# Late slots of three blocks and of one and a half in turn, and the low half of a weight split written one split later

## The chip, the cores and the metric

The kernel runs on one core of one Trainium2 chip. The metric is the device time of one execution in microseconds (us): 579.85 us is the median of three runs before the change (578.74 to 580.92). One further execution was recorded by the hardware profiler. It took 577.57 us, of which 575.6 us lie between the first and the last instruction; this is the span in which all positions below are given, counted from its start.

## The reference

Two stages follow each other. The first is an attention with memory: per batch and head, `phi` is softened over 32 memory columns, `k` and `v` are summed into 32 memory rows with these weights, and the 576 queries attend to the 32 rows. Its output is rearranged to 4608 tokens of 512 numbers. The second is a mixture of 8 experts: each token goes to the one expert with the highest gate value.

```python
e_idx = np.argmax(logits, axis=1)
...
for e in range(E):
    mask = e_idx == e
    h = np.maximum(x[mask] @ w1[e], 0.0)
    ye = h @ w2[e]
    out[mask] = gate_w[mask, None] * eom[mask, e, None] * ye
```

Here `x` is 4608 x 512, `w1[e]` 512 x 1024 and `w2[e]` 1024 x 512, all float32.

## The kernel before

**Slots.** Tokens are sorted by expert into blocks of 128, and blocks of one expert are put together in slots. A slot is a unit of work with one expert's weights. Five early slots (positions 0 to 4) hold three blocks each, from tokens whose attention is finished while attention still runs. The late slots are made when all tokens are routed: five of three blocks (positions 5 to 9), then four "of one and a half" (positions 10 to 13: one block of 128 tokens and a half of 64). Slots of one block exist in the program behind a condition on how many are in use; in the profiled execution none of them runs. Below, a slot of three blocks is called a *triple* and a slot of one and a half a *pair*, as the code's `nb == 3` and `nb == 2`.

**A slot on TensorE.** `several` does one slot. Its first layer runs over four weight tiles `u` = 0 to 3 (each 128 x 1024) and two halves `j`, its second layer over `u` = 4 to 7 and the blocks. Every float32 operand is split in two float32r parts, high and low: `xh` and `xl` for the tokens, `whl[:, 0]` and `whl[:, 1]` for the weights, `hh` and `hl` for the hidden values. A product is then the sum of three matmuls (high by high, low by high, high by low). A pair lays the 192 high and 192 low token columns side by side in one tile, so its first layer needs two matmuls, of 384 columns (line 1212) and of 256 columns (line 1213). After each `u` the sums are evacuated: for a triple by `hh` on ScalarE (line 1221) and `hl` on VectorE (line 1222); for a pair by a longer relay, two copies on ScalarE (1224), two additions on VectorE (1225), the relu on ScalarE (1229) and two subtractions on VectorE (1231).

**Weights.** `Stream` brings them: `fetch` starts the loads of 512 KB tiles on SyncE's queue (line 563) into `raw` buffers, `split` makes the high part by a cast on ScalarE (line 574) and the low part by a subtraction on VectorE (line 575) that needs the cast. The split tiles live in a ring, of ten buffers once attention is over (`settle` adds the last six). `done`, called once for each weight tile that has been used, issues up to two further splits (`PUMP[0]` is 2), so that splits run ahead of their use.

**Tokens.** `gathers` issues the gathering transfers on GpSimd for up to three slots ahead, twelve for a triple and six for a pair, each of a quarter of a row. `turn_x` prepares the tokens of the next slot during the second layer of the present one: four transposes on VectorE (line 1051), four casts to the high part on ScalarE (1058 for a pair, 1069 for a triple) and four subtractions on VectorE (1059 and 1070). The high part `xh` has one buffer, so its first write waits until the present slot's first layer is through.

**Order.** Each engine runs its instructions in the order in which the Python code emits them; nothing is rearranged later. The order of slots is the list `order`, and the place of every split, cast and subtraction in the queues of ScalarE and VectorE follows from where `done`, `nxt` and `hook` are called in `several`.

Of the kernel before, what the change touches and what calls it, by code (L numbers as in the profile page):

```python
# [7 lines left out]
F32 = mybir.dt.float32  # L8
# [4 lines left out]
ALU = mybir.AluOpType  # L13
# [15 lines left out]
NPT, NPP, NSS = 5, 4, 22  # L29
NPE = sum(NPS)  # L30
# [24 lines left out]
PUMP = (2, 1)  # L55
# [11 lines left out]
def attention_moe(tc, phiT, kv, qT, wgo, wall, out):  # L67
    nc = tc.nc
    V, A, G, T = nc.vector, nc.scalar, nc.gpsimd, nc.tensor

    with contextlib.ExitStack() as ctx:
# [385 lines left out]
        env = {}  # L457
# [18 lines left out]
        def force():  # L476
            clock[0] += 1
            (rou if rou.gens else late if late.gens else att).step()

        class Ring:  # L480


            def __init__(self, shape, dt, name):
                self.shape, self.dt, self.name = shape, dt, name
                self.pools, self.turn, self.size = [], [], 0
# [11 lines left out]
        raw = Ring([P, 1024], F32, "w")  # L497
# [5 lines left out]
        slots = []  # L503
        for s in range(NSLOT):
            nb = 3 if s < NPE + NPT else 2 if s < NPE + NPT + NPP else 1
# [3 lines left out]
            else:  # L509
                j = s - NPE  # L510
# [2 lines left out]
            slots.append({"s": s, "nb": nb, "q0": q0, "idx": idx[nm], "rows": rows,  # L513
                          "nm": nm, "quart": s not in WHOLE,
                          "known": False, "listed": False})
        order = slots

        def quarters(z, k):

# [24 lines left out]
        class Stream:  # L544
# [4 lines left out]
            def __init__(self, lo, hi):  # L549
                self.lo = lo  # L550
                self.fetched = self.parted = self.used = 8 * lo
                self.hi, self.w, self.hl = 8 * hi, {}, {}

            def fetch(self):
                while self.fetched < min(self.hi, self.parted + raw.size):
                    z = order[self.fetched // 8]
                    if not z["known"]:
                        return
                    if "e" not in z:
                        z["e"] = nc.sync.value_load(slot[0:1, z["s"]:z["s"] + 1], min_val=0, max_val=E - 1)  # L560
                    w = raw.tile()
                    u = self.fetched % 8
                    nc.sync.dma_start(w[:], wall[bass.ds(z["e"], 1), :, u + 8 * (z["quart"] and u < 4)])
                    self.w[self.fetched] = w
                    self.fetched += 1

            def split(self, ahead):

                self.fetch()
                m = self.parted  # L570
                if m == self.fetched or m >= self.used + ahead:
                    return False
                w, hl = self.w.pop(m), ring.tile()
                A.copy(hl[:, 0], w[:])  # L574
                V.tensor_tensor(hl[:, 1], w[:], hl[:, 0].bitcast(F32), ALU.subtract)  # L575
                self.hl[m] = hl
                self.parted += 1
                self.fetch()
                return True

            def take(self, i, u):
                m = 8 * i + u
                while m not in self.hl:
                    while not order[i]["known"]:
                        force()
                    assert self.split(ring.size)
                return self.hl[m]

            def done(self, n):
# [30 lines left out]
        def bank(shape, key="pa"):  # L620
            t = env[key].tile([P, 512], F32, name="b" + key)
            n = 1
            for x in shape:
                n *= x
            if len(shape) == 1:
                return t[:, 0:n]
            return t[:, 0:n].rearrange("p (a b) -> p a b", a=shape[0])
# [551 lines left out]
        def finish_y(z, k, py):  # L1179
            y = mo.tile([P, DM], F32, name="y", bufs=2)  # L1180
            n = P
            if (z["nb"], k) == (2, 1):

                n = 64
                ya = env["xt"].tile([64, DM], F32, name="ya", bufs=1)
                A.copy(ya[:], py[64:128])
                V.tensor_tensor(ya[:], py[0:64], ya[:], ALU.add)
                py = ya[:]
            A.activation(y[0:n], py[0:n], AF.Copy, scale=z["g"][0:n, k:k + 1] if z["quart"] else z["xg"][:, k, P:P + 1])  # L1189
            G.indirect_dma_start(  # L1190
                out=out, out_offset=bass.IndirectOffsetOnAxis(ap=z["idx"][1][0:n, z["q0"] + k:z["q0"] + k + 1], axis=0),
                in_=y[0:n], in_offset=None, bounds_check=NTOK - 1, oob_is_err=False)

        def several(i, st, nxt, hook):


            z = order[i]
            nb, x, h = z["nb"], z["x"], []
            n_ = nb * P
            for u in range(4):  # L1200
                w = st.take(i, u)
                h_ = mo.tile([P, 2, 3 * P], F32R, name="hh", bufs=4)
                l_ = mo.tile([P, 2, 3 * P], F32R, name="hl", bufs=4) if nb == 3 else None
                sh = mo.tile([P, 2, 192], F32, name="hl", bufs=4) if nb == 2 else None
                for j in range(2):
                    pb = bank([512], "ps")[:, 0:3 * P]
                    n = 0
                    for cc in range(4):
                        o = cc * 256 + j * P
                        if nb == 2:  # L1210

                            T.matmul(pb, w[:, 0, o:o + P], x[0][:, cc], start=(cc == 0), stop=False)  # L1212
                            T.matmul(pb[:, 0:256], w[:, 1, o:o + P], x[0][:, cc, 0:256],  # L1213
                                     start=False, stop=(cc == 3))
                            continue
                        for a, b in PASS:
                            T.matmul(pb, w[:, b, o:o + P], x[a][:, cc, 0:n_],  # L1217
                                     start=(n == 0), stop=(n == 11))
                            n += 1
                    if nb == 3:  # L1220
                        A.activation(h_[:, j], pb, AF.Relu)  # L1221
                        V.scalar_tensor_tensor(l_[:, j], pb, 0.0, h_[:, j].bitcast(F32), ALU.max, ALU.subtract)  # L1222
                    else:
                        A.copy(sh[:, j], pb[:, 192:384])
                        V.tensor_tensor(sh[:, j], pb[:, 0:192], sh[:, j], ALU.add)
                    if j == 0:
                        hook()
                if nb == 2:
                    A.activation(h_[:, :, 0:192], sh[:], AF.Relu)
                    for o, c, m in ((192, P, 64), (256, 0, P)):  # L1230
                        V.scalar_tensor_tensor(h_[:, :, o:o + m], sh[:, :, c:c + m], 0.0,
                                               h_[:, :, c:c + m].bitcast(F32), ALU.max, ALU.subtract)
                h.append((h_, l_))
                st.done(PUMP[0])
                hook()
            py = [bank([DM], "ps") for _ in range(nb)]

            turns = [(u, k) for u in range(4, 8) for k in range(nb)]
            if 8 * i + 8 == st.hi:
                turns.sort(key=lambda t: t[1], reverse=nb == 2)  # L1240
            for step, (u, k) in enumerate(turns):
                w = st.take(i, u)
                for f in range(2):
                    h_, l_ = h[u - 4]
                    if nb == 3:
                        ps = [((h_, l_)[a][:, f, k * P:(k + 1) * P], b) for a, b in PASS]
                    elif k == 0:
                        ps = [(h_[:, f, 256 * a:256 * a + P], b) for a, b in PASS]
                    else:
                        ps = [(h_[:, f, P:256], b) for b in range(2)]  # L1250
                    for n, (a, b) in enumerate(ps):
                        T.matmul(py[k], a, w[:, b, DM * f:DM * f + DM],  # L1252
                                 start=(u == 4 and f == 0 and n == 0),
                                 stop=(u == 7 and f == 1 and n == len(ps) - 1))
                if u == 7:
                    finish_y(z, k, py[k])
                hook()
                if step in TURN[nb]:
                    nxt(TURN[nb].index(step))
                if (step + 1) % nb == 0:  # L1260
                    st.done(PUMP[0])
# [159 lines left out]
```

## Time and profile before

| what | us |
|---|---|
| median of three runs | 579.85 |
| the profiled execution | 577.57 |
| its span | 575.6 |
| TensorE matmul busy in the span | 521.2 |
| VectorE busy | 363.1 |
| ScalarE busy | 288.6 |
| GpSimd busy | 225.6 |

"Busy" sums the time in which at least one instruction of an engine is under way. TensorE's matmuls overlap each other in its pipeline, so a matmul that is listed with 390 ns may follow the one before after 230 ns. The granted clock (PEclk) is 1.00 when TensorE runs at full speed. In the tables by stretches, each row gives the stretch, its length, and for each engine the busy time and the number of instructions; then the granted clock, the share of the DMA engines and GB/s. In rows by time the number in brackets is how long the engine sat idle before, and what released it.

### The profile page before, as it was taken

The page shows a single profiled execution, that of the slowest core. Times are in us where ns is not written, and L with a number is a line of the kernel's source. Part 1 is how long each engine was busy: PE and PEld are TensorE (multiplying, and loading weights), DVE is VectorE, ACT ScalarE, POOL GpSimd, SP SyncE. Part 2 cuts the span into 40 slices and gives each one's busy share as a digit, 9 for nine tenths or more (in the row PEclk, how much of TensorE's full clock was granted, in tenths as well). Part 3 has the DMA queues.
Part 4 walks back from the last instruction along what each step waited for, and adds up shares of the span by engine and source line. Part 5 has one row for each costly group of instructions (what it writes and reads, how often), then busy time and mean ns, then how long its engine had stood idle before and what let it go on. Part 6 is the DMA issues. An engine that isn't in the chain of part 4 may idle for free. (4 is left out here: it accounts for less than half of the span.)

```text
span 575.6 us, 10623 instructions
## 1 busy us (share of the span) xinstructions
PE 521.2 (91%) x3871; PEld 446.5 (78%) x3871; DVE 363.1 (63%) x791; ACT 288.6 (50%) x532; POOL 225.6 (39%) x245
## 2 busy tenths in 40 slices
PE   3788777789899999999999999999999999797894
PEld 2455555469689899898998989899898989696783
DVE  4485989767866559996353555647354545777750
ACT  3476664355345456543434545455453545666651
POOL 2242575740165034402471745547140505352011
PEclk9977989869999999999999999999999999898988
DMA  8999998985457759755564655646465564777101
GB/s 304 414 383 398 408 389 312 317 311 168 116 179 237 234 174 299 259 151 155 184 202 139 206 179 182 193 158 191 138 187 165 177 182 141 202 222 221 49 27 33
DMA packets 41853, 123.53 MB, mean 215 GB/s; under 512 B 10112, under 2 KB 10176, under 8 KB 41408
## 3 DMA queue, kind: packets, MB, share of 16 engines
q1 hardware_dynamic: 35136, 102.71, 55.1%
q0 software_dynamic: 6656, 20.06, 10.0%
q8 instruction: 32, 0.52, 0.4%
q14 instruction: 29, 0.24, 0.1%
HBM read 102.40 MB, written 20.35 MB: 213 GB/s over the span
## 5 line engine op out<-in xcount | busy, mean ns | idle before, releaser
L1252 PE MATMUL bps<-whl,hh 128*128 128x512 f32 x640 | 194.3, 394 | 0.0
L575 DVE TENSOR_TENSOR whl<-w,whl 128x1024 fp32r<-128x1024 f32 x112 | 136.9, 1228 | 66.1 <-ACT whl L574 65.7
L1217 PE MATMUL bps<-xh,whl 128*128 128x384 f32 x640 | 167.1, 338 | 0.0
L1252 PEld LDWEIGHTS bps<-whl,hh 128*128 128x128 f32 x640 | 119.9, 188 | 26.9 <-issue 2.5
L574 ACT CAST whl<-w 128x1024 fp32r<-128x1024 f32 x112 | 116.1, 1044 | 15.5 <-PE bps L1252 15.4
L1217 PEld LDWEIGHTS bps<-xh,whl 128*128 128x128 f32 x640 | 116.8, 189 | 1.2 <-issue 0.6
L1217 PE MATMUL bps<-xl,whl 128*128 128x384 f32 x320 | 107.6, 336 | 0.0
L1252 PE MATMUL bps<-whl,hl 128*128 128x512 f32 x240 | 93.7, 390 | 0.0
L529 POOL DMA_INDIRECT xg<-xs,idx_ql x72 | 84.3, 1171 | 21.9 <-issue 21.3
L1190 POOL DMA_INDIRECT out<-y,idx_ol x23 | 26.0, 1129 | 134.4 <-ACT y L1189 92.8
L1221 ACT ACTIVATE hh<-bps 128x384 fp32r<-128x384 f32 x80 | 39.3, 492 | 76.4 <-PE bps L1217 76.3
L1222 DVE SCALAR_TENSOR_TENSOR hl<-bps,hh 128x384 fp32r<-128x384 f32 x80 | 44.1, 554 | 38.4 <-ACT hh L1221 38.2
L1217 PEld LDWEIGHTS bps<-xl,whl 128*128 128x128 f32 x320 | 60.6, 189 | 0.4
L1212 PE MATMUL bps<-xh,whl 128*128 128x384 f32 x128 | 43.2, 372 | 9.6 <-DVE xh L1059 9.3
L1252 PEld LDWEIGHTS bps<-whl,hl 128*128 128x128 f32 x240 | 45.2, 188 | 8.4
L848 POOL TENSOR_TENSOR ea<-ea,mx 128x512 f32<-128x512 f32 (+1 forms) x20 | 19.2, 961 | 47.7 <-DVE mx L846 43.4
L1213 PE MATMUL bps<-xh,whl 128*128 128x256 f32 x128 | 37.8, 295 | 0.0
L1212 PEld LDWEIGHTS bps<-xh,whl 128*128 128x128 f32 x128 | 26.5, 207 | 12.6 <-DVE xh L1059 12.0
L883 ACT COPY xo<-bpd 128x576 f32<-128x576 f32 x36 | 22.6, 639 | 19.9 <-PE bpd L881 11.6
L966 POOL TENSOR_SCALAR Aw<-iota_row,row 128x128 bf16<-128x128 bf16 x36 | 26.9, 763 | 12.7 <-DVE row L956 12.7
L1189 ACT ACTIVATE y<-bps,xg 128x512 f32<-128x512 f32 x18 | 12.4, 689 | 35.3 <-PE bps L1252 14.5
L881 PE MATMUL bpd<-ve_b,aT 64*128 64x144 f32 (+1 forms) x320 | 27.8, 321 | 2.3 <-DVE ea L843 2.1
(264 smaller groups left out, 596.4 us busy)
## 6 DMA issues: line engine op xcount, KB each, us to landing
w<-wall SPq DMA_DIRECT2D x112, 512.0 KB, 4.0
kvt<-kv SPq DMA_DIRECT2D x32, 512.0 KB, 7.1
xs<-xo SPq DMA_DIRECT2D x16, 576.0 KB, 6.5
qt<-qT SPq DMA_DIRECT2D x16, 512.0 KB, 8.4
ph<-phiT SPq DMA_DIRECT2D x3, 1152.0 KB, 11.4
kv<-kv SPq DMA_DIRECT2D x4, 512.0 KB, 8.7
ph<-phiT SPq DMA_DIRECT2D x4, 288.0 KB, 3.2
xs<-xo SPq DMA_DIRECT2D x8, 144.0 KB, 4.9
```

Source lines behind the costliest of these rows:

```text
L529: G.indirect_dma_start(out=z["xg"][:, k, XQ * b:XQ * b + XQ], out_offset=None, in_=xs[0:z["rows"]].rearrange("t (a q) -> (t a) q", a=4), i ...
L574: A.copy(hl[:, 0], w[:])
L575: V.tensor_tensor(hl[:, 1], w[:], hl[:, 0].bitcast(F32), ALU.subtract)
L881: T.matmul(px[to:to + n, r, sl], z["aT"][h, o:o + n], ves[2 * bp + b][h, g], start=True, stop=True)
L966: (G if AWP else V).tensor_scalar(Aw[:, bp * NCH + c], iota_row[:], row[:, c:c + 1], None, ALU.is_equal)
L1190: G.indirect_dma_start(out=out, out_offset=bass.IndirectOffsetOnAxis(ap=z["idx"][1][0:n, z["q0"] + k:z["q0"] + k + 1], axis=0), in_=y[0:n] ...
L1212: T.matmul(pb, w[:, 0, o:o + P], x[0][:, cc], start=(cc == 0), stop=False)
L1213: T.matmul(pb[:, 0:256], w[:, 1, o:o + P], x[0][:, cc, 0:256], start=False, stop=(cc == 3))
L1217: T.matmul(pb, w[:, b, o:o + P], x[a][:, cc, 0:n_], start=(n == 0), stop=(n == 11))
L1221: A.activation(h_[:, j], pb, AF.Relu)
L1222: V.scalar_tensor_tensor(l_[:, j], pb, 0.0, h_[:, j].bitcast(F32), ALU.max, ALU.subtract)
L1252: T.matmul(py[k], a, w[:, b, DM * f:DM * f + DM], start=(u == 4 and f == 0 and n == 0), stop=(u == 7 and f == 1 and n == len(ps) - 1))
```

## The change

Three things change.

1. **The order of slots.** The five early slots stay. The late triples and the pairs now come in turn: triple, pair, triple, pair, and so on, with the fifth triple last. The slots themselves, their tokens and their experts are the same.
2. **The low part of a split.** Once attention is over (`"hs" in env`), a split casts its own tile and then subtracts for the tile before it; its own subtraction stays open until the next split, or until the tile is about to be used. One raw buffer more counts as taken while a subtraction is open.
3. **The place of the splits in a pair.** In a pair's first layer `done`, and so the casts and subtractions of its splits, now stands before the two subtractions of line 1231 (1248 in the new file), not after them.

```diff
-        order = slots
+        m = NPE + NPT
+        order = slots[:NPE]
+        for j in range(max(NPT, NPP)):
+            order += slots[NPE + j:NPE + j + 1] * (j < NPT) + slots[m + j:m + j + 1] * (j < NPP)
+        order += slots[m + NPP:]
...
-                while self.fetched < min(self.hi, self.parted + raw.size):
+                while self.fetched < min(self.hi, self.parted + raw.size - bool(self.half)):
...
                 A.copy(hl[:, 0], w[:])
-                V.tensor_tensor(hl[:, 1], w[:], hl[:, 0].bitcast(F32), ALU.subtract)
+                self.flush()
+                self.half = w, hl
                 self.hl[m] = hl
                 self.parted += 1
+                if "hs" not in env:
+                    self.flush()
                 self.fetch()
                 return True
+
+            def flush(self):
+
+                if self.half:
+                    w, hl = self.half
+                    V.tensor_tensor(hl[:, 1], w[:], hl[:, 0].bitcast(F32), ALU.subtract)
+                    self.half = None
...
+                if m + 1 == self.parted:
+                    self.flush()
                 return self.hl[m]
...
                 if nb == 2:
                     A.activation(h_[:, :, 0:192], sh[:], AF.Relu)
+                    st.done(PUMP[0])
                     for o, c, m in ((192, P, 64), (256, 0, P)):
                         V.scalar_tensor_tensor(h_[:, :, o:o + m], sh[:, :, c:c + m], 0.0,
                                                h_[:, :, c:c + m].bitcast(F32), ALU.max, ALU.subtract)
                 h.append((h_, l_))
-                st.done(PUMP[0])
+                if nb == 3:
+                    st.done(PUMP[0])
                 hook()
```

In the rows below each engine's instructions stand in the order of its queue, output before the arrow, with buffer numbers where they matter. The new file's lines are 16 to 18 higher there: 592 is the subtraction of line 575, 578 the cast of 574, 1240, 1241, 1245 and 1248 are 1224, 1225, 1229 and 1231, and 1067 and 1086 are 1051 and 1070.

VectorE, in a pair's first layer, before: one round for one `u`, from a split's subtraction to the next.

```order
L575 TENSOR_TENSOR whl<-w,whl 128x1024
L1225 TENSOR_TENSOR hl<-bps,hl 128x192 x2
L1231 SCALAR_TENSOR_TENSOR hh<-hl,hh 128x2x64
L1231 SCALAR_TENSOR_TENSOR hh<-hl,hh 128x2x128
L575 TENSOR_TENSOR whl<-w,whl 128x1024
```

ScalarE and then VectorE, in a pair's first layer, after, with the numbers of the buffers: one round on ScalarE, and the same round on VectorE.

```order
L578 CAST whl_4393<-w_4227 128x1024
L1240 COPY hl_4418<-bps_4419 128x192
L1240 COPY hl_4418<-bps_4430 128x192
L1245 ACTIVATE hh_4417<-hl_4418 128x2x192
L578 CAST whl_4442<-w_4264 128x1024
```

```order
L1241 TENSOR_TENSOR hl_4418<-bps_4419,hl_4418 128x192
L1241 TENSOR_TENSOR hl_4418<-bps_4430,hl_4418 128x192
L592 TENSOR_TENSOR whl_4393<-w_4227,whl_4393 128x1024
L1248 SCALAR_TENSOR_TENSOR hh_4417<-hl_4418,hh_4417 128x2x64
L1248 SCALAR_TENSOR_TENSOR hh_4417<-hl_4418,hh_4417 128x2x128
L1241 TENSOR_TENSOR hl_4450<-bps_4451,hl_4450 128x192
```

The subtraction for buffer 4393, cast at the head of the round, stood ahead of the additions into 4418; it now stands behind them, and behind it comes the pair of subtractions that finishes the round.

VectorE, in a pair's second layer, before, where the next slot is a pair: the tokens are turned (1051), cast on ScalarE and subtracted (1059) between the splits.

```order
L575 TENSOR_TENSOR whl<-w,whl 128x1024
L1051 STREAM_TRANSPOSE xt<-xg 128x192 x2
L1059 TENSOR_TENSOR xh<-xt,xh 128x192
L575 TENSOR_TENSOR whl<-w,whl 128x1024
L1051 STREAM_TRANSPOSE xt<-xg 128x192
L1059 TENSOR_TENSOR xh<-xt,xh 128x192
L1051 STREAM_TRANSPOSE xt<-xg 128x192
L1059 TENSOR_TENSOR xh<-xt,xh 128x192
L575 TENSOR_TENSOR whl<-w,whl 128x1024
L1059 TENSOR_TENSOR xh<-xt,xh 128x192
L575 TENSOR_TENSOR whl<-w,whl 128x1024
L1187 TENSOR_TENSOR ya<-bps,ya 64x512
```

The same place after, where the next slot is a triple:

```order
L1067 STREAM_TRANSPOSE xt<-xg 128x384 x2
L1086 TENSOR_TENSOR xl<-xt,xh 128x384
L592 TENSOR_TENSOR whl<-w,whl 128x1024
L1067 STREAM_TRANSPOSE xt<-xg 128x384
L1086 TENSOR_TENSOR xl<-xt,xh 128x384
L1067 STREAM_TRANSPOSE xt<-xg 128x384
L1086 TENSOR_TENSOR xl<-xt,xh 128x384
L592 TENSOR_TENSOR whl<-w,whl 128x1024
L1086 TENSOR_TENSOR xl<-xt,xh 128x384
L592 TENSOR_TENSOR whl<-w,whl 128x1024
L1203 TENSOR_TENSOR ya<-bps,ya 64x512
```

What a pair's second layer has to prepare is now a triple: tiles of 384 columns in place of 192. The split's subtraction that stood right ahead of the first transposes now stands ahead of the last round's two subtractions of line 1248.

More of the change, by code (lines that the diff above doesn't have):

```diff
@@ L551, in __init__ @@
                 self.fetched = self.parted = self.used = 8 * lo
-                self.hi, self.w, self.hl = 8 * hi, {}, {}
+                self.hi, self.w, self.hl, self.half = 8 * hi, {}, {}, None
             def fetch(self):
-                while self.fetched < min(self.hi, self.parted + raw.size):
+                while self.fetched < min(self.hi, self.parted + raw.size - bool(self.half)):
                     z = order[self.fetched // 8]
```

## The prediction

> **What bounds the kernel now.** I read the part from the first late slot to the end in a table by stretches, cut where the first matmul of each slot starts; from the sixth slot on that is one row for a slot, and the last row is what follows the last matmul. The page's first lines give the whole.
>
> ```profile
> span 575.6 us, 10623 instructions
> PE 521.2 (91%) x3871; PEld 446.5 (78%) x3871; DVE 363.1 (63%) x791; ACT 288.6 (50%) x532; POOL 225.6 (39%) x245
> ```
>
> ```profile
> core 0: us, PE busy (x) PEld busy (x) DVE busy (x) ACT busy (x) POOL busy (x), PEclk, DMA share, GB/s
> 312.16:345.19 33.03, 33.03 (x169) 30.18 (x168) 17.15 (x23) 16.14 (x27) 17.95 (x15) 1.00 0.58 175
> 345.19:378.22 33.03, 33.03 (x170) 30.18 (x168) 17.80 (x24) 16.14 (x27) 17.06 (x15) 1.00 0.60 178
> 378.22:411.24 33.02, 33.02 (x169) 30.18 (x168) 17.83 (x25) 16.09 (x27) 17.08 (x15) 1.00 0.60 179
> 411.24:444.27 33.03, 33.03 (x169) 30.18 (x168) 17.80 (x25) 16.10 (x27) 9.31 (x9) 1.00 0.57 165
> 444.27:477.30 33.03, 33.03 (x170) 30.18 (x168) 16.69 (x25) 15.38 (x27) 9.30 (x9) 1.00 0.54 165
> 477.30:495.89 18.59, 18.59 (x105) 16.73 (x104) 11.86 (x25) 10.77 (x24) 10.01 (x8) 1.00 0.62 183
> 495.89:519.88 23.99, 20.77 (x105) 18.34 (x105) 17.29 (x33) 15.36 (x32) 11.52 (x8) 0.93 0.71 208
> 519.88:543.73 23.85, 20.68 (x105) 18.27 (x105) 17.27 (x33) 15.22 (x32) 3.34 (x2) 0.93 0.51 150
> 543.73:567.76 24.03, 20.83 (x105) 18.14 (x104) 11.38 (x26) 10.83 (x23) 3.37 (x3) 0.93 0.09 24
> 567.76:575.60 7.84, 0.01 (x1) 0.00 (x0) 0.00 (x0) 0.69 (x1) 0.98 (x1) 0.78 0.11 40
> ```
>
> All five triples and the first pair are TensorE from end to end: busy for the whole stretch, at clock 1.00. No other engine can shorten them. The other three pairs do the same work as the first, in 23.99, 23.85 and 24.03 us instead of 18.59. What they lose is 5.40 + 5.26 + 5.44 = **16.1 us**. Of that 3.2 us in each is idle (23.99 - 20.77), and the rest, 2.2 us in each, is work at a lower clock. The waits of TensorE and its rows by time in the second pair show both.
>
> ```profile
> PE bps L1212 <- DVE xh L1059: 9.3, 6, 1.7
> ```
>
> ```profile
> 498.14 0.44 PE L1212 MATMUL bps<-xh,whl 128*128 128x384 f32 x1 [1.72 <-DVE xh L1059]
> 498.42 0.28 PE L1213 MATMUL bps<-xh,whl 128*128 128x256 f32 x1
> ...
> 500.76 0.69 PE L1212 MATMUL bps<-xh,whl 128*128 128x384 f32 x1 [1.40 <-DVE xh L1059]
> ```
>
> ```profile
> 496.43:500.76 4.33, 1.12 (x4) 0.59 (x4) 3.83 (x8) 3.00 (x6) 0.00 (x0) 0.97 0.67 217
> ...
> 501.00:501.80 0.80, 0.80 (x4) 0.80 (x5) 0.80 (x2) 0.57 (x1) 0.56 (x1) 0.50 0.84 82
> ```
>
> TensorE waits twice in each of these pairs for the tokens of its own slot (line 1059), six waits of together 9.3 us. After the second wait the granted clock is 0.50. So the tokens are late where the slot ahead is a pair, and are not where it is a triple. To see why they are late, ScalarE's and VectorE's rows in the first pair are needed.
>
> ```profile
> 480.16 0.54 ACT L1224 COPY hl<-bps 128x192 f32<-128x192 f32 x2
> 482.08 0.53 ACT L1229 ACTIVATE hh<-hl 128x384 fp32r<-128x384 f32 x1 [1.38 <-DVE hl L1225]
> 482.51 1.04 ACT L574 CAST whl<-w 128x1024 fp32r<-128x1024 f32 x1
> 483.46 0.53 ACT L1224 COPY hl<-bps 128x192 f32<-128x192 f32 x2
> 485.38 0.52 ACT L1229 ACTIVATE hh<-hl 128x384 fp32r<-128x384 f32 x1 [1.39 <-DVE hl L1225]
> 485.81 1.03 ACT L574 CAST whl<-w 128x1024 fp32r<-128x1024 f32 x1
> ...
> 491.96 0.53 ACT L1229 ACTIVATE hh<-hl 128x384 fp32r<-128x384 f32 x1 [1.39 <-DVE hl L1225]
> 492.39 1.04 ACT L574 CAST whl<-w 128x1024 fp32r<-128x1024 f32 x1
> 493.33 0.82 ACT L1044 COPY gx<-xg 32x2 f32<-32x2 f32 x4
> ```
>
> ```profile
> 483.58 1.23 DVE L575 TENSOR_TENSOR whl<-w,whl 128x1024 fp32r<-128x1024 f32 x1 [0.29 <-ACT whl L574]
> 484.73 0.61 DVE L1225 TENSOR_TENSOR hl<-bps,hl 128x192 f32<-128x192 f32 x2
> 485.93 0.63 DVE L1231 SCALAR_TENSOR_TENSOR hh<-hl,hh 128x128 fp32r<-128x128 f32 x2 [0.59 <-ACT hh L1229]
> ```
>
> A round on these two engines is one chain: cast at 482.51, the subtraction at 483.58 that needs it, the additions at 484.73 that stand behind it in VectorE's queue, the relu at 485.38 that needs them, the next cast at 485.81. That is 3.30 us a round. TensorE goes through the pair's first layer in a quarter of 18.59 - 9.21 = 9.4 us for each `u`, so 2.35 us:
>
> ```profile
> 486.68:495.89 9.21, 9.21 (x42) 7.35 (x41) 6.91 (x14) 5.50 (x15) 5.79 (x5) 1.00 0.72 214
> ```
>
> Four rounds of 3.3 us against four of 2.35: the engines come to the copies at 493.33, with which the next slot's tokens begin, only 2.56 us before the next slot starts at 495.89.
>
> **The change part by part.** Times are now counted from the start of a pair's first layer (477.30 in the trace). The first evacuation starts at 2.86 there and I keep it.
>
> *The round.* With the subtraction one split late, the additions of line 1225 wait only for ScalarE's copies. A round on ScalarE is the cast until its successor starts (483.46 - 482.51 = 0.95), the two copies (0.53), the second addition behind them (0.35 and some 0.05 to hand over), the relu until its successor (485.81 - 485.38 = 0.43): 2.3 us. VectorE has 1.15 (484.73 - 483.58) for a subtraction, 0.61 for the additions and about 0.57 for the two of line 1231: 2.33 us. TensorE sets 2.35. I take 2.4 us a round. The bounds are 2.3 and the old 3.3. The new place of `done` puts the split ahead of line 1231 and so lets VectorE subtract while ScalarE runs the relu, which the 0.59 idle in the last row above leaves free.
>
> First relu: 2.86 + 0.53 + 0.4 = 3.8 (was 4.8). Fourth: 3.8 + 3 x 2.4 = 11.0 (was 491.96 - 477.30 = 14.7). So the pair's relay ends **3.6 us earlier**, and the copies `gx` start at 11.0 + 0.43 + 0.95 = 12.4.
>
> *The tokens of a triple in a pair's second layer.* They are wider than before; the prices, by form, over the stretch 340 to 576:
>
> ```profile
> L1070 DVE TENSOR_TENSOR xl<-xt,xh 128x384 fp32r<-128x384 f32 x14 | 7.6, 540 | 18.3 <-ACT xh L1069 18.3
> L1051 DVE STREAM_TRANSPOSE xt<-xg 128x384 f32<-128x384 f32 x13 | 7.4, 572 | 0.0
> L1069 ACT CAST xh<-xt 128x384 fp32r<-128x384 f32 x14 | 7.1, 506 | 0.0
> ...
> L1051 DVE STREAM_TRANSPOSE xt<-xg 128x192 f32<-128x192 f32 x16 | 5.6, 366 | 0.1
> L1059 DVE TENSOR_TENSOR xh<-xt,xh 128x192 fp32r<-128x192 f32 x16 | 5.4, 339 | 5.2 <-ACT xh L1058 5.2
> ```
>
> Four transposes and four subtractions cost 4 x (0.572 + 0.540) = 4.4 us in place of 4 x (0.366 + 0.339) = 2.8: 1.6 us more on VectorE. Run through its queue, each instruction holding it about 0.08 less than its duration: the round's last subtractions end at 12.7; two transposes to 13.7; the first cast on ScalarE runs 13.2 to 13.7; first `xl` to 14.3; a split to 15.4; transpose to 15.9; second `xl` to 16.4; transpose to 16.9; third `xl` to 17.4 (its cast, 16.0 to 16.5, is done); a split to 18.5; fourth `xl` to **19.1**. TensorE starts the triple at 18.59 and needs the fourth `xl` after three steps and one matmul. A step is a thirty-second of the triple's first layer, 16.66 / 32 = 0.52 us:
>
> ```profile
> 378.22:394.88 16.66, 16.66 (x97) 16.66 (x96) 9.03 (x12) 7.77 (x12) 9.65 (x10) 1.00 0.59 174
> ```
>
> So it is needed at 18.59 + 3 x 0.52 + 0.17 = 20.3, which leaves 1.2 us. The four entries from pair to triple then cost nothing; what covers them is the pair's own second layer, and without the 3.6 us they would be late by 2.4.
>
> *The four entries from triple to pair.* The trace has one, at 477.30, without idle time. The triple's second layer lasts 33.03 - 16.66 = 16.4 us and carries less preparation. Cost: nothing, four times.
>
> *The splits, one late.* The weights are far ahead. Of 112 casts 24 come after 479, three slots' worth, when TensorE has just begun the eleventh of fourteen slots:
>
> ```profile
> 479.00:576.00 97.00, 24.90 (x24) 0.93 0.44 130
> ...
> 0.00:223.41 223.41, 25.64 (x25) 0.92 0.82 291
> ```
>
> Even soon after attention, at 223.41, where TensorE begins the fifth tile of the third slot (the 21st in all), 25 are cast. A subtraction that comes one pair of splits later (some 4 us) stays ahead. The raw buffer held longer delays a load by as much, and the DMA engines are busy 0.71 of the time at most in these slots. Cost: nothing; if the lead were gone, up to 1.2 us for each tile.
>
> *Moved transfers.* A triple's twelve gathers and three stores take GpSimd 17 to 18 us and now always fall into a triple's 33.03; a pair's eight instructions take 10.0 of 18.59. They are issued two slots ahead, as before. One load of weights goes behind four small stores on SyncE's queue, early, where the lead covers it. The end (7.84 us after the last matmul: the same scale, store and wait) is the same for a triple.
>
> *Sum.* From 312.16: 5 x 33.03 + 4 x 18.59 = 239.5 us instead of 567.76 - 312.16 = 255.6. The profiled execution (577.57, its span 575.6) falls by 16.1 to 561.5. The median of the runs is 2.3 above that execution, so 579.85 - 16.1 = 563.8. I add 0.2 for what four entries may lose at their edges: **564.0 us**.
>
> One rule speaks to the clock. The Trainium skill ("TensorE: Matmul & The Clock Gate", sections "What's actually happening" and "Why this matters for your kernels") says that the array falls to half rate after about one idle window of 3.4 us and that gaps below some 3 us are safe. The row with 0.50 agrees on the half; on the gap it differs, since here 1.72 and 1.40 us with four matmuls between were enough, so the trace decides. By the rule these entries would lose 9.6 us of idle time alone and the sum would be 570.3.
>
> **The rivals.**
>
> *A (slower): the relay keeps its length.* If the round stays near 3.3 us, because VectorE's queue or the relu's wait holds it at some other place, the tokens of each triple are 2.4 us late at the least, and with the 2.2 us at lower clock an entry costs 4.6; at the pairs' own price 5.4. There are four such entries now, not three: 4 x 4.6 to 4 x 5.4 against 16.1 gives 2.3 to 5.5 us more, 582 to 585; I price it at **584**. For it: VectorE is the fuller engine in the pairs (17.29 of 23.99) and has 1.6 us more to do. Against it: every idle stretch in the relay's rows has a named end that the new order removes. It decides once the tokens come 3.0 us later than in my schedule (then 1.8 idle and 2.2 clock, 4.0 an entry, is what is saved).
>
> *B: part of the delay stays.* If they come 2.4 us later, one split's subtraction and one transpose or two, each entry idles 1.2 us. A first gap of 1.72 us was followed by matmuls 0.28 us apart and clock 0.97, so no loss of clock: 4 x 1.2 = 4.8, **568.8**. For it: 1.2 us of slack over a schedule of some twenty instructions is little.
>
> *C: nothing is gained.* The late tokens aren't set by the relay but by the gathers landing, or the loads, and the wait only moves to other slots: **579**. Against it: the gathers for a pair are issued two slots ahead, and the row at 493.33 follows the cast before it without a gap.
>
> **How the numbers follow.** The forecast has 0.75, B 0.13, A 0.08, C 0.04. What this measurement can tell from no change is about 0.5%, 2.9 us. Forecast and B are faster by more than that, and so is what lies between: 0.88. C is the same, with a little of A: 0.05. The rest of A is slower: 0.07. The range goes from all 16.1 us gained, less the 1.1 us by which the runs shown lie from their median (562.5), to somewhat beyond B (570); it leaves out A and C, and a little of B.
>
> **What would show it.** In the changed kernel's table every triple after attention should take 33.0 us and every pair 18.6, at clock 1.00, and TensorE should have no wait on line 1075 or 1086 (the new lines of 1059 and 1070) longer than 0.3 us. In a pair's first layer ScalarE's casts should come 2.4 us apart, and the copies `gx` about 12.4 us after its start. Rival A would show rounds of 3.3 us and waits at the start of each triple that follows a pair, with clock 0.5 behind them; B such waits with clock 1.00. If pairs take 18.6 us but the span falls by less, something before 312 us has changed, which I hold for nothing.

## The result, and the profile after

The changed kernel takes 562.21 us (median of four runs, 560.33 to 563.20), the kernel before 579.30 in the same comparison. The ratio is 0.9697 with a 95% interval of 0.9661 to 0.9734: 3.0% faster. A second comparison of the same two kernels (told below) gave 561.39 and 0.9702 (0.9673 to 0.9731). The forecast was 564.0 in a range of 562.5 to 570.0, so the direction and the size were right and the range missed by 0.3 us, at its lower end.

The profiled execution took 563.06 us, its span is 561.3. The table by stretches, cut where the first matmul of each late slot starts (triple, pair, triple, ...), last row behind the last matmul:

```profile
314.45:347.47 33.02, 33.02 (x169) 30.18 (x168) 14.56 (x23) 15.38 (x27) 17.23 (x15) 1.00 0.56 175
347.47:365.93 18.46, 18.46 (x106) 16.89 (x105) 16.16 (x31) 14.24 (x29) 9.61 (x8) 1.00 0.74 226
365.93:398.95 33.02, 33.02 (x169) 30.18 (x168) 17.97 (x28) 16.94 (x30) 17.51 (x15) 1.00 0.67 206
398.95:417.41 18.46, 18.46 (x106) 16.89 (x105) 16.15 (x32) 14.29 (x29) 9.86 (x8) 1.00 0.73 229
...
501.91:520.37 18.46, 18.46 (x106) 16.89 (x105) 16.06 (x31) 14.25 (x29) 2.25 (x2) 1.00 0.44 130
520.37:553.56 33.19, 33.18 (x169) 29.99 (x167) 7.91 (x13) 7.57 (x14) 4.19 (x4) 1.00 0.09 29
553.56:561.30 7.74, 0.00 (x0) 0.00 (x0) 0.00 (x0) 0.69 (x1) 0.97 (x1) 0.63 0.12 40
```

The dots stand for two more triples and a pair, with the same times. Every late slot is now TensorE from end to end at clock 1.00, the triples 33.0 us and the pairs 18.46. The last triple's 33.19 holds the end of its last matmul, which nothing follows. From the first late slot to the last matmul it is 553.56 - 314.45 = 239.1 us where it was 255.6. The profile lists no wait of TensorE there.

ScalarE's and VectorE's rows in the first pair (347.47 to 365.93) answer to those shown of before:

```profile
350.35 0.54 ACT L1240 COPY hl<-bps 128x192 f32<-128x192 f32 x2
351.36 0.52 ACT L1245 ACTIVATE hh<-hl 128x384 fp32r<-128x384 f32 x1 [0.47 <-DVE hl L1241]
351.79 1.04 ACT L578 CAST whl<-w 128x1024 fp32r<-128x1024 f32 x1
352.74 0.53 ACT L1240 COPY hl<-bps 128x192 f32<-128x192 f32 x2
353.73 0.53 ACT L1245 ACTIVATE hh<-hl 128x384 fp32r<-128x384 f32 x1 [0.47 <-DVE hl L1241]
354.16 1.04 ACT L578 CAST whl<-w 128x1024 fp32r<-128x1024 f32 x1
...
358.46 0.53 ACT L1245 ACTIVATE hh<-hl 128x384 fp32r<-128x384 f32 x1 [0.47 <-DVE hl L1241]
358.89 1.04 ACT L578 CAST whl<-w 128x1024 fp32r<-128x1024 f32 x1
359.83 0.84 ACT L1060 COPY gx<-xg 32x3 f32<-32x3 f32 x4
```

```profile
350.71 0.62 DVE L1241 TENSOR_TENSOR hl<-bps,hl 128x192 f32<-128x192 f32 x2 [1.89 <-ACT hl L1240]
351.25 1.22 DVE L592 TENSOR_TENSOR whl<-w,whl 128x1024 fp32r<-128x1024 f32 x1
352.38 0.62 DVE L1248 SCALAR_TENSOR_TENSOR hh<-hl,hh 128x128 fp32r<-128x128 f32 x2
...
365.97 0.55 DVE L1086 TENSOR_TENSOR xl<-xt,xh 128x384 fp32r<-128x384 f32 x1
```

The relu waits 0.47 us for the additions, not 1.39; VectorE goes from the additions to the split's subtraction to line 1248 without idling. Casts are 354.16 - 351.79 = 2.37 us apart. The last row is the fourth `xl` of the triple: it ends 19.05 us after the pair's start. TensorE uses it at 20.2:

```profile
367.34 0.51 PE L1233 MATMUL bps<-xh,whl 128*128 128x384 f32 x2
367.69 0.33 PE L1233 MATMUL bps<-xl,whl 128*128 128x384 f32 x1
```

so 1.17 us are left.

### The profile page after: what moved, and what is told of

Read it like the earlier page. It is cut to its first block, busy times and chain, and to the rows that moved or that the text cites. A ratio compares the mean times of both kernels' runs of the same rounds, so it can differ in the third digit from the quotient of the medians.

```text
span 561.3 us, 10581 instructions
## 1 busy us (share of the span) xinstructions
PE 514.2 (92%) x3871; PEld 442.2 (79%) x3871; DVE 358.8 (64%) x791; ACT 287.1 (51%) x532; POOL 226.0 (40%) x245
## 5 line engine op out<-in xcount | busy, mean ns | idle before, releaser
L1233 PE MATMUL bps<-xh,whl 128*128 128x384 f32 x640 | 166.9, 337 | 0.0
L1233 PEld LDWEIGHTS bps<-xh,whl 128*128 128x128 f32 x640 | 116.6, 189 | 1.7 <-issue 0.6
L1228 PE MATMUL bps<-xh,whl 128*128 128x384 f32 x128 | 37.7, 338 | 0.0
L1229 PE MATMUL bps<-xh,whl 128*128 128x256 f32 x128 | 35.7, 279 | 0.0
L1205 ACT ACTIVATE y<-bps,xg 128x512 f32<-128x512 f32 x18 | 12.4, 688 | 33.1 <-PE bps L1270 14.0
L1206 POOL DMA_INDIRECT out<-y,idx_ob x9 | 11.4, 1270 | 43.5 <-ACT y L1205 33.6
```

The source lines that it names most:

```text
L1206: G.indirect_dma_start(out=out, out_offset=bass.IndirectOffsetOnAxis(ap=z["idx"][1][0:n, z["q0"] + k:z["q0"] + k + 1], axis=0), in_=y[0:n] ...
L1233: T.matmul(pb, w[:, b, o:o + P], x[a][:, cc, 0:n_], start=(n == 0), stop=(n == 11))
```

## The experiments

Two explanations stood against each other. *R*: the relay between ScalarE and VectorE in a pair's first layer sets when the next slot's tokens come. *O*: it is the order of slots, since a pair's second layer is too short to prepare another pair right behind a pair. All edits below are to the changed kernel.

### The order alone, the relay alone

The order alone, with the relay as before:

```diff
-                if "hs" not in env:
-                    self.flush()
+                self.flush()
...
-                    st.done(PUMP[0])
                     for o, c, m in ((192, P, 64), (256, 0, P)):
...
-                if nb == 3:
-                    st.done(PUMP[0])
+                st.done(PUMP[0])
```

> The slots in turn, but each split subtracts for its own tile at once and stands behind line 1231's subtractions, as in the kernel before. Theory R (the relay between ScalarE and VectorE in a pair's first layer sets when the next slot's tokens come): rounds stay at 3.3 us, the fourth relu ends 3.6 us later than in the changed kernel, each of the four triples behind a pair waits about 2.4 us and then works some 2.2 us longer at a lower clock: 4.6 to 5.4 us an entry, 18 to 22 us against the changed kernel's 562.2, so 580 to 584 us, a little slower than before. Rival O (it is the order: a pair's second layer is too short to prepare for another pair right after a pair, and a triple gives the room back): 562 to 566 us, triples of 33.0 us.

Measured: 588.15 us (586.66 to 588.42), ratio 1.016 (1.0122 to 1.0198), 1.6% slower than before. The relay has its old length, and each triple behind a pair waits, then runs at half clock (ScalarE in the first pair; the waits; the first such triple, and a stretch in it):

```profile
350.93 1.03 ACT L578 CAST whl<-w 128x1024 fp32r<-128x1024 f32 x1
...
354.22 1.03 ACT L578 CAST whl<-w 128x1024 fp32r<-128x1024 f32 x1
```

```profile
PE bps L1232 <- DVE xl L1085: 8.8, 13, 1.3
```

```profile
364.17:404.12 39.95, 37.22 (x169) 32.80 (x169) 23.47 (x34) 20.85 (x35) 18.15 (x15) 0.91 0.66 190
369.50:376.40 6.90, 6.26 (x21) 6.26 (x22) 4.56 (x7) 4.91 (x8) 1.53 (x1) 0.54 0.73 202
```

Casts are 3.29 us apart. The triple takes 39.95 us and not 33.02; the other three 39.7 to 39.8. Four entries lose some 27 us where three lost 16.

The relay alone, in the old order:

```diff
-        m = NPE + NPT
-        order = slots[:NPE]
-        for j in range(max(NPT, NPP)):
-            order += slots[NPE + j:NPE + j + 1] * (j < NPT) + slots[m + j:m + j + 1] * (j < NPP)
-        order += slots[m + NPP:]
+        order = slots
```

> The slots in the old order (all triples, then all pairs), with the late subtraction and the new place of the splits. Theory R: the rounds are 2.4 us, the tokens of a pair are ready still earlier than a triple's (1.6 us less VectorE work), all four pairs take 18.5 us at clock 1.00: 562 us, the same as the changed kernel within 0.5%. Rival O: pairs behind pairs still take about 24 us, 578 to 580 us.

Measured: 561.20 us (560.04 to 564.80), ratio 0.9692 (0.9657 to 0.9727). That is the changed kernel's time. Its four pairs behind each other:

```profile
480.86:499.31 18.45, 18.45 (x105) 16.89 (x104) 15.92 (x33) 14.51 (x30) 10.38 (x8) 1.00 0.76 233
499.31:517.76 18.45, 18.45 (x105) 16.89 (x104) 16.34 (x34) 14.89 (x32) 10.75 (x8) 1.00 0.88 266
517.76:536.22 18.46, 18.46 (x105) 16.89 (x104) 16.49 (x34) 15.04 (x32) 2.18 (x3) 1.00 0.57 180
536.22:555.35 19.13, 18.92 (x105) 16.62 (x103) 8.45 (x20) 7.62 (x18) 2.87 (x3) 1.00 0.10 29
```

A pair behind a pair loses nothing once the relay is short. Only the last shows a wait, of 0.21 us, and it is not for tokens:

```profile
548.93 1.42 PE L1266 MATMUL bps<-whl,hh 128*128 128x512 f32 x5 [0.21 <-DVE whl L588]
```

Line 588 is the subtraction of a split there. The last tile's stays open until the tile is about to be used, and so it comes late; it accounts for some 0.5 us of the 19.13, the rest being the end of the last matmul. In the changed kernel a triple is last, and this wait does not appear. O falls: the order brings no gain that these runs can tell, and on its own it costs.

### The two halves of the relay's edit

With the slots in turn, the late subtraction but `done` at its old place, behind line 1231's subtractions (the lower two hunks of the order alone):

> The slots in turn and the late subtraction, but the splits of a pair's first layer stand behind line 1231's subtractions as before. Theory R: a round on VectorE is then one chain of the additions 0.61, the relu's wait 0.55, the two subtractions of line 1231 0.57 and the split's subtraction 1.15, 2.9 us, between the old 3.3 and the new 2.4; the tokens come 1.5 to 2 us later than in the changed kernel, which is 0.3 to 0.8 us more than their slack of 1.2: 564 to 568 us, or up to 575 if the clock falls behind such waits as well. Rival O: 562 us.

Measured: 566.47 us (564.83 to 567.78), ratio 0.9789 (0.9748 to 0.9830). VectorE's subtractions in a pair are 2.88 us apart, and a triple behind a pair takes 34.2 us:

```profile
357.73 1.22 DVE L592 TENSOR_TENSOR whl<-w,whl 128x1024 fp32r<-128x1024 f32 x1
...
360.61 1.22 DVE L592 TENSOR_TENSOR whl<-w,whl 128x1024 fp32r<-128x1024 f32 x1
```

```profile
365.42:399.66 34.24, 33.50 (x169) 30.09 (x168) 20.07 (x31) 19.06 (x33) 17.33 (x15) 1.00 0.67 209
```

The other half, `done` at its new place but each split subtracting at once (the first hunk of the order alone):

> The slots in turn and the splits ahead of line 1231, but each split subtracts for its own tile at once. Theory R: the cast, the subtraction that waits for it, line 1231's subtractions behind it, the additions and the relu are one chain of about 0.43 + 1.04 + 1.15 + 0.57 + 0.65 = 3.85 us a round, longer than before the change; the tokens come at least 4.4 us later than in the changed kernel, each triple behind a pair loses 3.2 us idle and 2.2 or more by the clock, and the pair's own second layer may wait for its hidden values: 584 to 592 us, slower than before. Rival O: 562 to 566 us.

Measured: 589.12 us (586.53 to 589.88), ratio 1.0177 (1.0131 to 1.0222), slower than before. The round is 3.83 us (expected 3.85), and now the pair's second layer waits for its own hidden values (line 1247) as well as the triple for its tokens:

```profile
352.52 1.03 ACT L578 CAST whl<-w 128x1024 fp32r<-128x1024 f32 x1
...
356.35 1.03 ACT L578 CAST whl<-w 128x1024 fp32r<-128x1024 f32 x1
```

```profile
PE bps L1269 <- DVE hh L1247: 10.0, 8, 1.3
PE bps L1232 <- DVE xl L1085: 9.1, 12, 1.2
```

```profile
347.32:369.10 21.78, 19.24 (x106) 16.64 (x105) 12.27 (x26) 11.59 (x25) 9.66 (x8) 1.00 0.57 176
369.10:405.30 36.20, 33.89 (x170) 30.04 (x169) 22.51 (x33) 19.47 (x34) 18.01 (x15) 1.00 0.66 197
```

Here the expectation was right on the whole by luck and wrong in its parts: the clock stayed at 1.00, and the pair's own 3.3 us came in its place. The fair comparison for this half is the order alone, which has the same slots: its round was 3.29 us and its time 588.15 (586.66 to 588.42). So without the late subtraction the new place of `done` makes the round longer, and the time no different that these runs can tell. This half in the old order was not run.

The late subtraction alone, in the old order, with `done` at its old place:

> The old order and the old place of the splits in a pair, with the late subtraction alone. Theory R: a round is 2.9 us, as with the slots in turn and the late subtraction (357.73 to 360.61 there); the tokens of a pair need 1.6 us less of VectorE than a triple's, but TensorE goes through them faster and needs the last at 18.46 + 3 x 0.29 = 19.3 us instead of 20.2, so 0 to 0.8 us lost at each of three entries: 561 to 564 us, the late subtraction alone carries nearly all of the gain. Against it, if the place of the splits matters for itself: pairs of 20 us and more, 567 us or more.

Measured: 566.85 us (566.05 to 568.65), ratio 0.9789 (0.9758 to 0.9819). That is outside the 561 to 564 us expected, and next to the 567 of the other explanation. The pairs take 18.45, 18.92, 20.69 and 21.27 us; these are the first and the third:

```profile
479.77:498.22 18.45, 18.45 (x105) 16.89 (x104) 13.99 (x31) 12.54 (x27) 9.98 (x8) 1.00 0.70 208
...
517.14:537.83 20.69, 19.29 (x105) 16.91 (x104) 16.86 (x34) 15.27 (x32) 3.14 (x3) 1.00 0.62 199
```

I had taken each entry by itself. With a round of 2.9 against TensorE's 2.35 a pair ends late, and in a row of pairs the next begins with that lateness: the copies `gx` start 13.9, 16.1 and 17.8 us after the start of the first, second and third pair. So the place of the splits does matter, by way of the round. With the slots in turn the same relay lost 1.1 to 1.2 us at each of four entries. From the first late slot to the last matmul that is 243.7 us in turn and 244.5 in the old order, against 239.1 with the short round. So the order matters little whichever relay of 2.4 or 2.9 us goes with it.

### How much slack there is

The first transpose of each triple behind a pair is done several times over, with the same result:

```diff
-                    V.transpose(xt[:, 0:m].rearrange("p (k i) -> p k i", i=32),
-                                xg[:, 0:nb].rearrange("p k (b q) -> p (k b) q", b=4)[:, 0:m // 32, 32 * c:32 * c + 32])
+                    for _ in range(1 + 2 * (nb == 3 and c == 0)):
+                        V.transpose(xt[:, 0:m].rearrange("p (k i) -> p k i", i=32),
+                                    xg[:, 0:nb].rearrange("p k (b q) -> p (k b) q", b=4)[:, 0:m // 32, 32 * c:32 * c + 32])
```

> The changed kernel with the first transpose of each triple behind a pair done three times over instead of once: VectorE comes 2 x 0.49 = 1.0 us later to what follows, the results are the same. In the changed kernel the last tokens are ready 1.17 us before TensorE needs them. Theory R: no wait, triples of 33.0 us. If the slack is less than the schedule says: up to 1 us a triple more, 34 us.

Measured: triples of 33.15 to 33.25 us behind pairs (33.34 at the end, for 33.19), 0.13 to 0.23 us more; the one execution took 564.77 us. An extra transpose costs more than the 0.49 us expected. The first two of a triple take 1.03 us in the changed kernel (first row); with two more they take 2.25 (second row), so 0.61 us each. The fourth `xl` (third row) ends 368.99 - 348.74 = 20.25 us after its pair's start, where it was 19.05, so the delay was 1.2 us and used the slack of 1.17 up:

```profile
360.02 1.03 DVE L1067 STREAM_TRANSPOSE xt<-xg 128x384 f32<-128x384 f32 x2
```

```profile
361.28 2.25 DVE L1068 STREAM_TRANSPOSE xt<-xg 128x384 f32<-128x384 f32 x4
368.44 0.55 DVE L1087 TENSOR_TENSOR xl<-xt,xh 128x384 fp32r<-128x384 f32 x1
```

The same with five more transposes in place of two:

> The same with the first transpose done six times over: VectorE comes 5 x 0.49 = 2.45 us later, 1.3 us past the slack. Theory R: one wait in each of four triples, 1.3 to 1.8 us each with TensorE's pipeline to fill again, at clock 1.00, since the wait of 0.75 us (with late subtraction alone) had no loss of clock: triples of 34.3 to 34.8, 5 to 7 us in all. If a wait of this length already lowers the clock: triples of 37 to 38 us with rows at 0.50, 16 to 20 us in all.

Measured: 571.59 us (one execution), triples of 35.0 to 35.2 us behind pairs, 2.0 us more each, at clock 1.00. The wait of 0.75 us that the expectation names is that of the run with the slots in turn and the late subtraction. The fourth `xl` ends 22.10 us after its pair's start, so the delay is 3.05 us and 1.9 past the slack, which is what a triple lost. The first such triple:

```profile
366.12:401.22 35.10, 33.90 (x169) 30.05 (x168) 20.90 (x33) 19.30 (x33) 17.10 (x15) 1.00 0.65 202
```

And with nine more:

> The changed kernel with the first transpose of each triple behind a pair done ten times over: VectorE comes 9 x 0.49 = 4.4 us later, 3.3 us past the slack, twice and a half the lateness of the run with 2.45. If idle time of this length within some 5 us lowers the clock, as the slots in turn alone had it (triples of 39.8 us, clock 0.54 for 6.9 us): triples of 39 to 41 us with rows at 0.50. If the clock was lowered there for another reason: 3.3 us idle and 0.7 to fill the pipeline again, triples of 37 us at clock 1.00.

Measured: 588.64 us (one execution). The delay is 5.5 us by the fourth `xl`, so 4.3 past the slack. A triple takes 38.7 to 39.0 us, and the pair ahead of it 0.7 to 0.8 more than before, since the triple's first cast is already late for its start: together 57.9 us where they took 51.5. The rows are the first such triple and stretches in it:

```profile
366.37:405.04 38.67, 37.24 (x169) 32.76 (x170) 22.70 (x34) 20.80 (x35) 16.84 (x15) 0.91 0.60 183
366.40:369.40 3.00, 1.84 (x5) 1.01 (x6) 2.97 (x5) 2.11 (x4) 0.00 (x0) 0.95 0.16 18
369.40:372.80 3.40, 3.12 (x9) 2.31 (x9) 3.40 (x6) 3.15 (x5) 0.56 (x1) 0.50 0.56 164
372.80:376.20 3.40, 3.40 (x13) 3.40 (x13) 2.24 (x3) 2.15 (x3) 0.85 (x1) 0.54 0.83 243
```

Lateness alone, with nothing else changed, thus gives back the whole gain and more, about half of it through the clock (0.91 over 38.67 us is some 3.5 us, of 6.5 lost by the two slots). It stays at 0.50 to 0.54 for 6.8 us, much as with the order alone.

### The scatter of the early part

The changed kernel once more:

> The changed kernel once more, for the scatter between executions. If the time up to the sixth slot scatters by itself (312.2 to 315.7 us in the six profiles so far, whose programs agree nearly up to there) and the late part does not: the sixth slot again anywhere between 312 and 316, the slots behind it 33.02 and 18.46 us to 0.1 us, a median of 561 to 563 us. If the change itself moved the early part by 2 us: again at 314 or later.

Measured: 561.39 us (560.54 to 561.91). Its profiled execution took 560.54 and reached the first late slot at 311.7, 2.7 us earlier than the first profile of the same program; the late part is the same to 0.1 us. The kernel before once more:

> The kernel before once more. If the time up to the sixth slot scatters by itself: the sixth slot anywhere between 311.7 and 315.7 us, as in the ten profiles so far, and the late part as before, 33.03 us for a triple and 18.6 and 24.0 for the pairs. If the kernel before reaches its sixth slot earlier than the changed one: at 312 again.

Measured: 577.04 us (one execution), first late slot at 311.7, then 33.02 to 33.03 a triple and 18.59, 23.96, 23.86 and 24.08 for the pairs. Over the twelve profiles the first late slot begins between 311.7 and 315.7: at 312.2 and 311.7 in the two of the kernel before, at 314.5 and 311.7 in the two of the changed kernel, and up to 315.7 in the runs with parts of the edit. Since the same program gave both 314.5 and 311.7, the difference need not come from the change; two profiles of the kernel before are few to say how far it scatters by itself. The scatter lies ahead of the third slot; the rows are the changed kernel (first profile, then second) from the first slot's start to the third's and on to the first late slot:

```profile
122.82:208.63 85.81, 83.45 (x543) 70.98 (x544) 56.21 (x138) 38.24 (x62) 28.48 (x31) 0.96 0.61 191
208.63:314.45 105.82, 105.82 (x592) 95.65 (x591) 74.45 (x170) 51.50 (x76) 34.32 (x30) 1.00 0.63 194
```

```profile
121.20:205.90 84.70, 82.34 (x546) 70.27 (x545) 55.95 (x138) 38.35 (x63) 27.70 (x31) 0.98 0.61 192
205.90:311.70 105.80, 105.80 (x591) 95.65 (x590) 74.40 (x170) 51.31 (x76) 33.82 (x30) 1.00 0.63 194
```

What makes it scatter was not tried.

## Why the prediction was right, and where its range failed

**What bounds the kernel** was right: the loss was 5.3 to 5.4 us at three entries from pair to pair, and it was the lateness of the tokens. The runs with extra transposes show it from the other side. One row was read wrongly: the first pair, 18.59, was not TensorE from end to end. The weight load of the next pair's first matmul came 0.37 us after the load before it, at 495.86, just behind the first subtraction of that pair's tokens (495.39 + 0.36):

```profile
495.86 0.19 PEld L1212 LDWEIGHTS bps<-xh,whl 128*128 128x128 f32 x1 [0.37 <-issue]
```

```profile
495.39 0.36 DVE L1059 TENSOR_TENSOR xh<-xt,xh 128x192 fp32r<-128x192 f32 x1 [0.16 <-ACT xh L1058]
```

In the changed kernel the same load ahead of the triple at 365.93 has no idle time before it (365.70). So the 0.13 us by which this pair exceeds 18.46 is most likely lateness too; the trace names no releaser for it.

**The round** was right nearly to the hundredth. Forecast 2.4 us, measured 2.37. Fourth relu 11.0 us after the pair's start, measured 358.46 - 347.47 = 10.99; copies `gx` 12.4, measured 12.36; fourth `xl` 19.1, measured 19.05. Both edits are needed for it: rounds of 2.9 us without the new place of `done`, 3.8 without the late subtraction, 3.3 without either.

**The entries from triple to pair and the splits** cost nothing, as forecast; in the old order one open subtraction costs some 0.5 us at the very end. Nor did the moved transfers cost anything, though the DMA engines were busy up to 0.75 of a pair and not 0.71.

**The sum** was a little short. The late stretch fell by 255.6 - 239.1 = 16.5 us and the end by 0.1, where I had 16.1. The term that was mis-sized is the pair, 18.59 in the only row that I had and 18.46 in all four of now, 0.5 us together, less 0.1 that the last triple's end took back. The 0.2 us that I added for the entries' edges were not there. With the end these make 0.7 of the 1.8 us between 564.0 and 562.2.

**The step that failed is the base and the range's lower end.** I took 579.85, the median of three runs, as the kernel before, and the 1.1 us by which those runs lie from it as all the scatter there is (which gives 562.65, where I wrote 562.5). In the comparison with the result the kernel before had 579.30, which is another 0.55 of the 1.8 us; in the later ones it had 579.05 and 578.91. The last 0.5 lies within the scatter: the medians fell by 17.1 us here and by 17.5 in the second comparison, the profiles' late part and end by 16.6. Either the measured base or the measured gain in place of mine would have put 562.21 inside the range. With both, 1.1 us would still have been too narrow for the second median, 561.39. The early part, which the change hardly touches, moves by up to 4 us between executions, and the numbers that I had could have told me: the profiled execution of before was 2.3 us faster than the median. The gain of the late part should have been forecast as 16 to 17 us, and the time as 562.5 with 2 us either way.

**Rival A** did not come, but the order alone showed its mechanism, and at a higher price: 588 us and not 584. The idle time was about as scheduled: 2.3 us of waits an entry, where I had 2.4. The clock's part was mis-sized: 0.91 over 39.95 us is some 3.6 us lost, with 6.9 us near half rate, where I had taken 2.2 from a pair before the change. Even there 0.93 over 23.99 us accounts for only some 1.7 of the 2.2. **Rival B** was priced about right: with 1.9 us of lateness past the slack an entry lost 2.0 us, at clock 1.00. The lateness decides, not the idle time in the rows: in the run with the late subtraction and the order the last tokens came 1.0 us after their need (368.23 - 346.97 = 21.26 us after the pair's start, against 20.22), the wait in the rows was 0.75 us, and the triple lost 1.1 to 1.2. **Rival C** is excluded by the time.

**What I did not forecast** is that the order of slots brings nothing. I costed the three edits as one change; the run without the order gives the same time. My schedule had the means to say it: a pair's tokens need 1.6 us less of VectorE than a triple's, so a short relay makes them ready in time as well.

## What to carry to other kernels

Where two in-order engines pass work back and forth, put an instruction that waits for the other engine's newest result one round later, so that it never stands ahead of work whose inputs are ready; and check its place against each neighbour, since half of such an edit can make the round longer than none (3.83 us against 3.29, and 2.37 with both halves). Here a reordering that gave the same engines room added nothing once the lateness was cured at its source, so cost each part of a change alone. When the profile and the median differ by as much as the allowance for scatter, the scatter belongs in the range.

## What the runs showed of the hardware that was not expected

The granted clock did not follow the length of single gaps. In the kernel before, waits of 1.72 and 1.40 us, four matmuls between, brought 0.50 for some 3 us. With the order alone, where no wait was above 1.34 us, it was 0.54 for 6.9 us; with ten transposes in place of one, where none was above 0.9, it was 0.50 to 0.54 for 6.8 us. With each split subtracting at once, triples with waits up to 1.2 us behind a pair that had waited twice 1.3 us itself kept clock 1.00. What decides between these is left open; the Trainium skill ("TensorE: Matmul & The Clock Gate", section "Why this matters for your kernels") gives gaps of about 3 us as the bound, and no single wait of TensorE in the late slots of these runs was longer than 1.73 us.
